# Where the attention matmuls stand among the feed-forward matmuls of the group before

## The chip, the cores and the metric

The kernel runs on one core of a Trainium2 chip. The core has five engines, each with its own in-order instruction queue: PE (TensorE, matrix multiply), DVE (VectorE), ACT (ScalarE), POOL (GpSimd) and SP (SyncE, which issues most of the DMAs). Time is device microseconds (us) of one execution, and lower is better. A scheduler writes the order of each engine's queue before the program runs. On the chip an engine takes its instructions in that order, and one that waits holds up everything queued behind it.

## The reference

A linear attention with a complex decay per channel is followed by a two-layer feed-forward block:

```python
for t in range(S):                       # S = 768, batch 4, heads 8, head_dim 48
    S_re, S_im = ar*S_re - ai*S_im + k[t] (x) v[t], ar*S_im + ai*S_re
    y[t] = q[t] @ S_re                   # a_re, a_im are first scaled to magnitude <= 0.999
x = y as (3072 tokens, 384 channels)
h = x @ w_in                             # 384 x 2048
out = max(0.01*h, h) @ w_out             # 2048 x 384
```

All data is float32, and the arrays w_in and w_out enter the kernel as float64 words.

## The kernel before, in words

The 768 positions are cut into 6 chunks of 128 tokens. One chunk of two batches is a *pass*, so there are 12 passes, numbered 0 to 11 (`SUBS`). For each pass the kernel does three things.

*Prep* (lines 438 to 611) is elementwise work on DVE and ACT: the magnitudes, the running products of the decay (lines 489 and 492, then 506 to 513), and their application to q and k. It writes `qkt`. Line 533 is the first write into the `qkt` of a pass and line 584, done twice, is the last. Ten DMAs (lines 600, 604 and 608) then carry `qkt` into `t96`, in a layout by head; the profile and its rows call this tile `t`. There is one `qkt` and one `t96` for all passes. So line 533 of the next prep has to wait until the DMAs have read `qkt`, and the DMAs of a pass have to wait until the attention of the pass before has finished with `t96`; its last reader there is the scaling of the state on ACT, line 729. In passes 0 and 1 five of the ten DMAs are issued by ACT, later all ten by SP.

*Attention* (`attend`, lines 632 to 733) has four pieces for a pass, scores and update for each of the two batches. A scores piece multiplies on PE from `t96` into PSUM; DVE then masks the result twice (line 670, tile `asb`). An update piece multiplies `asb` and the state into the attention's result, which ACT and DVE split into a high and a low part (`xh`, line 698, and `xl`, line 701), and updates the state (lines 722 and 729).

*Feed-forward* works on *groups* of 256 tokens, one for each pass. `first(g, s)`, for s from 0 to 7, is 18 matmuls into a PSUM tile `ph` (of which there are two), after which ACT, DVE, ACT and DVE make `tg`, `gh` and `gl` (lines 752 to 755). `second(g, s)` is 18 matmuls of `gh` and `gl` into `po`. Below, each such call of 18 matmuls is called a *step*, so a group has 16 steps. After the last, ACT copies `po` to `ot`, which SP stores (line 779).

While the feed-forward of group n-1 runs, the attention of pass n is put in between. The order on PE is fixed: every matmul is told to keep the order in which the program names it (`mm`, line 307). That order is made by this loop, in which `order` is the list of the steps of group n-1 and `pieces` the four attention pieces of pass n:

```python
805         if n > 0:
806             order = stream(n - 1)
807             for i, (what, g, s) in enumerate(order):
808                 what(g, s)
809                 left = len(order) - 1 - i
810                 while pieces and left <= GAP * len(pieces) + TAIL[min(n, len(TAIL) - 1)]:
811                     pieces.pop(0)()
812                     if left > 0:
813                         break
...
817         for p in pieces:
818             p()
```

`stream(g)` gives first 0, 1, 2, then second s-3 and first s alternating, then the last seconds. For groups 2 to 10 the last two seconds (6 and 7) are put behind first 0 of the next group. With `GAP` 2 the four pieces are issued two steps apart, and `TAIL[n]` says how many steps before the end of the group they begin. A value of -100 is never reached, so that the four pieces come after the last step of the group.

On the other engines the scheduler decides. It takes what is ready by its own simulation, attention before feed-forward before prep (`PRIO_ATT`, `PRIO_MOE`, `PRIO_PREP`), and fixes the order that comes out. In the first passes the weights are also converted, on DVE, ACT and POOL (`load_weights`, lines 406 to 434). In the last passes the weights are read once more and checked (`check_weights`, lines 392 to 404, tiles `wck`).

Of the kernel before, what the change touches and what calls it, by code (L numbers as in the profile page):

```python
# [42 lines left out]
OVERLAP = range(2, 11)  # L43

GAP = 2
TAIL = [0, -100, -100, 0, 2]
STAGES = [
    ("a", 3 * TI * 2 * C, 2), ("kn", H * 2 * D, 1), ("xh", TI * GT, 2), ("xl", TI * GT, 2), ("xh", TI * GT, 2),
    ("xl", TI * GT, 2), ("stg", 2 * DM, 1),
# [231 lines left out]
def body(ctx, tc, keep, a_in, qk_in, v_in, w_in, out):  # L281
# [512 lines left out]
    for n in range(nsub + 1):  # L794
# [10 lines left out]
        if n > 0:  # L805
            order = stream(n - 1)
            for i, (what, g, s) in enumerate(order):
                what(g, s)
                left = len(order) - 1 - i
                while pieces and left <= GAP * len(pieces) + TAIL[min(n, len(TAIL) - 1)]:  # L810
                    pieces.pop(0)()
# [86 lines left out]
```

## Time and profile before

| | us |
|---|---|
| median of 3 runs | 708.95 |
| lowest and highest | 705.37, 710.87 |
| the profiled execution | 711.76 |
| its span | 710.0 |
| PE busy | 563.7 (79%) |
| DVE busy | 550.4 (78%) |
| ACT busy | 366.2 (52%) |
| POOL busy | 79.2 (11%) |

The span is what the profiler saw between the first and the last instruction, and the profiled execution is 1.8 us longer than it. It lies 2.8 us above the median of the runs. A row of the timeline gives the start, the duration, the engine, the line, the operation and the count, and in brackets the idle time of that engine just before, with what ended it. A row of the waits gives who waited for whom, the sum, the number of times and the longest. A row of the windows gives the busy time of PE, of its weight load, of DVE, ACT and POOL in that stretch, the granted clock of PE as a share of full speed (PEclk), and the share of DMA time.

### The profile page before, as it was taken

The page shows a single profiled execution, that of the slowest core. Times are in us where ns is not written, and L with a number is a line of the kernel's source. Part 1 is how long each engine was busy: PE and PEld are TensorE (multiplying, and loading weights), DVE is VectorE, ACT ScalarE, POOL GpSimd, SP SyncE. Part 2 cuts the span into 40 slices and gives each one's busy share as a digit, 9 for nine tenths or more (in the row PEclk, how much of TensorE's full clock was granted, in tenths as well). Part 3 has the DMA queues.
Part 4 walks back from the last instruction along what each step waited for, and adds up shares of the span by engine and source line. Part 5 has one row for each costly group of instructions (what it writes and reads, how often), then busy time and mean ns, then how long its engine had stood idle before and what let it go on. Part 6 is the DMA issues. An engine that isn't in the chain of part 4 may idle for free.

```text
span 710.0 us, 17654 instructions
## 1 busy us (share of the span) xinstructions
PE 563.7 (79%) x7554; PEld 542.9 (76%) x7554; DVE 550.4 (78%) x917; ACT 366.2 (52%) x827; POOL 79.2 (11%) x75
## 2 busy tenths in 40 slices
PE   1000448966979889899899998998999979879996
PEld 0000338855978879889899998998999979879996
DVE  5999899999799599699896997969969767233331
ACT  6354276446453555464644755546456557554331
POOL 5645344630000000000000000000000000000000
PEclk9999956967989999999999999999999998989999
DMA  9222832720803503508025053160350674781000
GB/s 340 84 90 66 240 118 94 163 107 24 225 3 113 140 2 143 110 2 222 29 98 132 24 171 81 48 182 24 115 116 24 222 189 152 209 268 42 23 1 28
DMA packets 26247, 79.22 MB, mean 112 GB/s; under 512 B 3377, under 2 KB 9521, under 8 KB 26161
## 3 DMA queue, kind: packets, MB, share of 16 engines
q1 hardware_dynamic: 25552, 76.43, 36.3%
q10 hardware_dynamic: 608, 1.59, 1.0%
q8 instruction: 61, 1.00, 0.6%
q14 instruction: 26, 0.20, 0.1%
HBM read 54.26 MB, written 4.72 MB: 83 GB/s over the span
## 4 chain that ended last, share of the span: by engine, by line
DVE 41%; DMA 19%; PE 19%; ACT 7%; issue 7%; SPq 5%; POOL 1%; DVEq 0%; ACTq 0%
DMA t<-qkt 12%; PE po L308 8%; PE ph L308 6%; DMA wck<-in_w_dram 5%; PE att L308 4%; DVE tmp L489 3%; DVE gl L755 3%; DVE tg L753 3%; DVE asb L670 3%; DVE a L538 3%; ACT rst L729 2%; DVE a L492 2%; SPq L600 2%; DVE wcv L424 2%; SPq L604 2%
## 5 line engine op out<-in xcount | busy, mean ns | idle before, releaser
L308 PE MATMUL ph<-xh,win_hi 128*128 128x256 f32 x576 | 172.7, 300 | 26.8 <-DVE tg L753 20.0
L308 PE MATMUL ph<-xl,win_hi 128*128 128x256 f32 x576 | 167.7, 291 | 3.4 <-DVE xl L701 3.4
L308 PE MATMUL ph<-xh,win_lo 128*128 128x256 f32 x576 | 167.3, 290 | 2.0 <-POOL win_lo L434 2.0
L308 PE MATMUL po<-gh,wout_hi 128*128 128x256 f32 x576 | 144.0, 285 | 5.9 <-ACT ot L778 3.8
L308 PE MATMUL po<-gh,wout_lo 128*128 128x256 f32 x576 | 143.3, 284 | 0.0
L308 PEld LDWEIGHTS ph<-xh,win_hi 128*128 128x128 f32 x576 | 113.8, 198 | 31.9 <-DVE tg L753 22.0
L308 PEld LDWEIGHTS ph<-xl,win_hi 128*128 128x128 f32 x576 | 113.9, 198 | 4.2 <-DVE xl L701 4.2
L308 PEld LDWEIGHTS po<-gh,wout_hi 128*128 128x128 f32 x576 | 111.1, 193 | 6.5 <-ACT ot L778 4.0
L308 PEld LDWEIGHTS ph<-xh,win_lo 128*128 128x128 f32 x576 | 113.9, 198 | 2.5 <-POOL win_lo L434 2.5
L308 PEld LDWEIGHTS po<-gh,wout_lo 128*128 128x128 f32 x576 | 111.2, 193 | 0.0
L753 DVE TENSOR_TENSOR tg<-ph,tg 128x512 f32<-128x512 f32 x96 | 65.5, 684 | 48.8 <-ACT tg L752 46.2
L308 PE MATMUL att<-t 96*32 96x96 f32 (+3 forms) x1536 | 40.7, 261 | 76.3 <-DMA t<-qkt 73.4
L308 PEld LDWEIGHTS att<-t 96*32 96x32 f32 x1536 | 35.8, 146 | 80.6 <-DVE a L492 72.5
L754 ACT CAST gh<-tg 128x512 fp32r<-128x512 f32 x96 | 59.2, 617 | 53.8 <-DVE tg L753 50.9
L308 PE MATMUL po<-gl,wout_hi 128*128 128x256 f32 x576 | 84.5, 282 | 1.9 <-DVE gl L755 1.6
L755 DVE TENSOR_TENSOR gl<-tg,gh 128x512 fp32r<-128x512 f32 x96 | 68.2, 711 | 22.7 <-ACT gh L754 22.5
L752 ACT ACTIVATE tg<-ph 128x512 f32<-128x512 f32 x96 | 56.5, 589 | 43.2 <-PE ph L308 40.3
L308 PEld LDWEIGHTS po<-gl,wout_hi 128*128 128x128 f32 x576 | 75.5, 190 | 2.7 <-DVE gl L755 2.7
L533 DVE TENSOR_TENSOR qkt<-a 128x1536 f32<-128x1536 f32 x12 | 22.4, 1869 | 43.6 <-DMA t<-qkt 36.7
L489 DVE TENSOR_TENSOR tmp<-a 128x384 f32<-128x384 f32 x84 | 52.2, 622 | 1.3
L308 PE MATMUL att<-asb,v 128*32 128x128 f32 x768 | 43.3, 312 | 8.8 <-DVE asb L670 8.6
L729 ACT ACTIVATE rst<-rst,t 96x48 f32<-96x48 f32 x128 | 30.7, 323 | 20.2 <-DVE rst L722 20.1
(119 smaller groups left out, 898.9 us busy)
## 6 DMA issues: line engine op xcount, KB each, us to landing
t<-qkt SPq DMA_DIRECT2D x44, 290.2 KB, 6.0
wck<-in_w_dram SPq DMA_DIRECT2D x10, 1152.0 KB, 5.6
v<-in_v_dram SPq DMA_DIRECT2D x12, 832.0 KB, 4.7
a<-in_a_dram SPq DMA_DIRECT2D x12, 768.0 KB, 5.9
qk<-in_qk_dram SPq DMA_DIRECT2D x12, 768.0 KB, 4.4
out_dram<-ot SPq DMA_DIRECT2D x12, 384.0 KB, 2.6
stage_xh<-in_w_dram SPq DMA_DIRECT2D x10, 384.0 KB, 3.6
stage_xl<-in_w_dram SPq DMA_DIRECT2D x10, 384.0 KB, 3.0
```

Source lines behind the costliest of these rows:

```text
L308: tc.keep_in_program_order(nc.tensor.matmul(out, **kw))
L424: nc.vector.tensor_scalar(out=cv.bitcast(U32), in0=uwords[:, :, 1], scalar1=5, scalar2=2, op0=ALU.logical_shift_left, op1=ALU.logical_shif ...
L489: nc.vector.tensor_tensor(out=pr, in0=src.unsqueeze(2).to_broadcast([P, 2, 2, M]), in1=swap(ar, r), op=ALU.mult)
L492: nc.vector.tensor_tensor(out=zr[:, :, r], in0=pr[:, 0], in1=pr[:, 1], op=ALU.add)
L533: nc.vector.tensor_tensor(out=tb.rearrange("p l (r m) -> p l r m", r=R), in0=zl.rearrange("p l (r m) -> p l r m", r=R), in1=xt[:, 1].rearr ...
L538: nc.vector.tensor_tensor(out=zk, in0=zk, in1=over_r(0), op=ALU.mult)
L670: nc.vector.tensor_tensor(out=asb, in0=ps, in1=mask, op=ALU.mult)
L729: nc.scalar.activation(r[:, h // 2, h % 2], src[:, h // 2, h % 2], AF.Copy, scale=t96[:, s0 + x, bi, C : C + 1])
L752: nc.scalar.activation(tg, ph, AF.Copy, scale=0.01)
L753: nc.vector.tensor_tensor(out=tg, in0=ph, in1=tg, op=ALU.max)
L754: nc.scalar.copy(gh, tg)
L755: nc.vector.tensor_tensor(out=gl, in0=tg, in1=gh.bitcast(F32), op=ALU.subtract)
```

## The change

One line is changed, the table `TAIL`:

```diff
-TAIL = [0, -100, -100, 0, 2]
+TAIL = [1]
```

The table has one entry now, so every pass uses the value 1. This moves matmuls in all passes but pass 0:

- Passes 1 and 2: the four pieces stood behind all 16 steps of groups 0 and 1. They now stand after the steps with 9, 7, 5 and 3 steps left, which are first 4, 5, 6 and 7.
- Pass 3: they stood with 8, 6, 4 and 2 steps left, after second 1 to 4 of group 2, and now stand after first 3 to 6, one step earlier.
- Passes 4 to 11: they stood with 10, 8, 6 and 4 steps left, after second 0 to 3, and now stand after first 3 to 6, one step later.

No instruction's work changes. The order on the engines changes with the order on PE, since the scheduler works it out anew. Three places are shown, with a minus for a row of the kernel before, a plus for a row of the changed one.

The first is on DVE in the middle of group 0. The tile `a_2` belongs to the prep of pass 2, `wcv` to the weights, `tg_0_5` and `gl_0_5` to step first 5 of group 0, and `asb_1_0_0` is the first mask multiply of pass 1:

```order
 L755 TENSOR_TENSOR gl_0_4_928<-tg_0_4_926,gh_0_4_927 128x512
 L492 TENSOR_TENSOR a_2_756<-tmp_2_1318 128x2x96
-L753 TENSOR_TENSOR tg_0_5_970<-ph_0_5_951,tg_0_5_970 128x512
 L489 TENSOR_TENSOR tmp_2_1318<-a_2_756 128x384
 L492 TENSOR_TENSOR a_2_756<-tmp_2_1318 128x2x96
+L670 TENSOR_TENSOR asb_1_0_0_949<-att1_100,mask_78 128x512
 L489 TENSOR_TENSOR tmp_2_1318<-a_2_756 128x384
 L424 TENSOR_SCALAR wcv_30_457<-stage_stg_8_131 128x384
-L755 TENSOR_TENSOR gl_0_5_972<-tg_0_5_970,gh_0_5_971 128x512
 L492 TENSOR_TENSOR a_2_756<-tmp_2_1318 128x2x96
```

The mask multiply of pass 1 now stands where the feed-forward's step 5 stood, ahead of the last weights and of the rest of prep 2.

The second is on SP, the loads and stores around the `t96` of passes 2 and 3 (`ot` are the results of a group, `qk`, `a` and `v` the inputs of a pass):

```order
 L379 DMA a_3_1398<-in_a_dram 128x1536
-L779 DMA out_0_dram<-ot_0_1119 128x3x256
-L384 DMA qk_3_1399<-in_qk_dram 128x1536
-L379 DMA a_4_2074<-in_a_dram 128x1536
 L387 DMA v_2_758<-in_v_dram 128x1664
+L779 DMA out_0_dram<-ot_0_1313 128x3x256
 L600 DMA t96_2_1387<-qkt_2_1360 48x1548 x2
 L604 DMA t96_2_1387<-qkt_2_1360 32x2x516
```

The loads of `qk` and `a` that stood ahead of the DMAs into `t96` now stand behind them, and the store of group 0 stays ahead of those of pass 2. For pass 3 the store of group 1 now stands between the first two of the ten and the rest.

The third is on DVE around line 533 of prep 7, which runs beside group 5. Before:

```order
L512 TENSOR_TENSOR xs_7_4683<-tmp_7_4657 128x48
L513 TENSOR_TENSOR xs_7_4683<-tmp_7_4657 128x48
L533 TENSOR_TENSOR qkt_7_4699<-a_7_4061 128x2x768
L469 SCALAR_TENSOR_TENSOR tmp_8_5333<-tmp_8_5333 128x768
L753 TENSOR_TENSOR tg_5_0_4088<-ph_5_0_4069,tg_5_0_4088 128x512
L538 TENSOR_TENSOR a_7_4061<-a_7_4061 128x1536
L755 TENSOR_TENSOR gl_5_0_4090<-tg_5_0_4088,gh_5_0_4089 128x512
```

And now:

```order
L753 TENSOR_TENSOR tg_5_2_4181<-ph_5_2_4162,tg_5_2_4181 128x512
L506 TENSOR_TENSOR tmp_7_4657<-xs_7_4683 128x192
L512 TENSOR_TENSOR xs_7_4683<-tmp_7_4657 128x48
L513 TENSOR_TENSOR xs_7_4683<-tmp_7_4657 128x48
L755 TENSOR_TENSOR gl_5_2_4183<-tg_5_2_4181,gh_5_2_4182 128x512
L533 TENSOR_TENSOR qkt_7_4699<-a_7_4061 128x2x768
L469 SCALAR_TENSOR_TENSOR tmp_8_5333<-tmp_8_5333 128x768
L670 TENSOR_TENSOR asb_6_0_0_4251<-att1_100,mask_78 128x512
L538 TENSOR_TENSOR a_7_4061<-a_7_4061 128x1536
L753 TENSOR_TENSOR tg_5_3_4228<-ph_5_3_4209,tg_5_3_4228 128x512
```

The DVE work of firsts 0, 1 and 2 of group 5 (`tg` and `gl`), which was queued behind line 533, now stands ahead of it, and the mask multiplies of pass 6 (`asb_6`) stand two instructions behind it.

## The prediction

> **What bounds the kernel now.** The page comes first, then the windows by stage.
>
> ```profile
> PE 563.7 (79%) x7554; PEld 542.9 (76%) x7554; DVE 550.4 (78%) x917; ACT 366.2 (52%) x827; POOL 79.2 (11%) x75
> 100.00:180.00 80.00, 59.74 (x662) 55.98 (x655) 78.70 (x114) 45.02 (x106) 27.72 (x22) 0.74 0.33 98
> 372.00:560.00 188.00, 181.51 (x2637) 176.90 (x2636) 162.01 (x282) 103.30 (x246) 0.00 (x0) 0.99 0.35 99
> ```
>
> Over the whole span PE and DVE look alike, but the stages differ. From 100 to 180 us DVE is busy 78.7 of 80 us and PE 59.7: DVE bounds there, with the weights, prep 2 and the feed-forward of group 0. From 372 to 560 us PE is busy 181.5 of 188 us, 97%, and DVE 162.0, 86%: PE bounds there, with small gaps. The waits over the whole program tell what makes the gaps:
>
> ```profile
> DVE qkt L533 <- DMA t<-qkt: 36.7, 8, 5.7
> PE ph L308 <- DVE tg L753: 20.0, 10, 3.9
> ```
>
> Eight times DVE stands at line 533 until the DMAs into `t96` have read `qkt`. What is queued behind line 533 waits too, a `tg` among it, and PE then waits for that `tg` before it may refill a `ph`. The timeline of PE dates the stages. The rows are starts: scores of pass 1, group 1, scores of pass 2, group 2, scores of passes 3, 4, 8, 9 and 10.
>
> ```profile
> 160.74 0.50 PE L308 MATMUL att<-t 96*32 96x128 f32 x11
> 178.41 0.58 PE L308 MATMUL ph<-xh,win_hi 128*128 128x256 f32 x1
> 221.34 0.33 PE L308 MATMUL att<-t 96*32 96x128 f32 x4
> 235.26 0.38 PE L308 MATMUL ph<-xh,win_hi 128*128 128x256 f32 x1
> 250.73 0.33 PE L308 MATMUL att<-t 96*32 96x128 f32 x4
> 296.01 0.33 PE L308 MATMUL att<-t 96*32 96x128 f32 x4
> 489.35 0.33 PE L308 MATMUL att<-t 96*32 96x128 f32 x4
> 534.81 0.33 PE L308 MATMUL att<-t 96*32 96x128 f32 x4
> 581.76 0.35 PE L308 MATMUL att<-t 96*32 96x128 f32 x6
> ...
> 208.66 2.13 PE ph L308 x18
> 210.80 2.12 PE po L308 x18
> ```
>
> The last two rows are from the chain of waits: an undisturbed step is 2.13 us. From one pass's scores to the next (16 steps and an attention) the kernel takes 45.46 us at its best (489.35 to 534.81). From the start of group 1 to that of group 2, the same work, it takes 56.85 (178.41 to 235.26). From scores 4 to scores 10 it takes 285.75, which is 47.6 a pass. What the change can win lies in these two differences: 11.4 us early, 2.2 us a pass later.
>
> **The change, place by place.** I follow the new order with durations of the rows. The sum is made against the profiled execution, 711.8 us.
>
> *Scores of pass 1 inside group 0.* PE now comes to them after first 4, where it began second 2 before.
>
> ```profile
> 129.06 0.28 PE L308 MATMUL po<-gh,wout_hi 128*128 128x256 f32 x1
> 139.34 0.59 ACTq L608 DMA_DIRECT2D t<-qkt  x1
> t<-qkt ACTq DMA_DIRECT2D x4, 32.2 KB, 4.7
> 139.72 0.36 DVE L492 TENSOR_TENSOR a<-tmp 128x192 f32<-128x192 f32 x1
> 80.23 2.50 PE L308 MATMUL att<-t 96*32 96x64 f32 x56 [1.37 <-DMA t<-qkt]
> 176.27 1.82 DVE L584 TENSOR_TENSOR qkt<-qk,a 128x768 f32<-128x768 f32 x2
> L701 DVE SCALAR_TENSOR_TENSOR xl<-att,xh 128x384 fp32r<-128x384 f32 x24 | 13.2, 549 | 6.7 <-ACT xh L698 6.7
> ```
>
> PE is there at 129.1. The last DMA into this `t96` is issued at 139.3 and lands, by the median, 4.7 later, at 144.0. So PE stands for 14.9 us, with the rest of group 0 queued behind. DVE comes to the new mask multiply at 139.4 (the L492 row's end less the 0.68 of the `tg` that is no longer ahead) and finds it ready at 145.3 (half a cold scores piece, 2.50/2, after the landing). It stands for 5.9 us, and prep 2 and the last weights are queued behind. DVE has no slack here, so they end later by this. Up to line 584 of prep 2 both orders hold the same steps' `tg` and `gl` and four mask multiplies; the new one has one L701 more, 0.5. Line 584 ends at 178.0 before (the row holds most of both calls), and so at 184.4.
>
> The last `gl` of group 0 stands seven short DVE rows, some 4.4 us, ahead of that end. So second 7 ends and group 1 starts at about 180.7, 2.3 later than before, but with no attention left to do alone behind group 1.
>
> *Scores of pass 2 inside group 1.* After seven steps and 0.7 us of wait for a `tg`, PE is there at 196.3.
>
> ```profile
> 196.83 1.76 DVE L533 TENSOR_TENSOR qkt<-a 128x1536 f32<-128x1536 f32 x1 [5.65 <-DMA t<-qkt]
> 218.88 1.81 DVE L584 TENSOR_TENSOR qkt<-qk,a 128x768 f32<-128x768 f32 x2
> 222.34 0.69 DVE L670 TENSOR_TENSOR asb<-att,mask 128x512 f32<-128x512 f32 x1 [1.37 <-PE att L308]
> 238.60 2.56 SPq L600 DMA_DIRECT2D t<-qkt  x2
> 249.38 1.76 DVE L533 TENSOR_TENSOR qkt<-a 128x1536 f32<-128x1536 f32 x1 [3.43 <-DMA t<-qkt]
> L670 DVE TENSOR_TENSOR asb<-att,mask 128x512 f32<-128x512 f32 x48 | 31.7, 680 | 5.4 <-PE att L308 5.4
> L722 DVE TENSOR_TENSOR rst<-att,rst 96x384 f32<-96x384 f32 x16 | 8.7, 544 | 0.0
> ```
>
> From the first issue of the ten DMAs (238.60) to the end of the wait at line 533 (249.38) are 10.8 us. Issued at 184.4, those of pass 2 land at 195.2, just ahead of PE: no wait. Their place on SP helps, since two loads that stood ahead now stand behind; what could hold them is the store of group 0, which is ready by 181.5. Group 1 with attention 2 inside is then one undisturbed pass, 45.46 less the 1.0 of wait in it: 180.7 + 0.7 + 44.5 = 225.9 is the start of group 2, against 235.26.
>
> *Scores of pass 3.* Prep 3 is next to be late. Between the ends of line 584 of preps 2 and 3 lie 42.7 us before, with 5.65 of idle at line 533. The new order puts four L670, one more L701 and two L722 in, 4.4, and I add one wait for scores like that at 222.34, 1.4. The idle goes: 184.4 + 42.7 - 5.65 + 4.4 + 1.4 = 227.2. The store of group 1 between its DMAs costs 0.4; landing is at 238.4. PE is there five steps after 225.9, at 236.5, and waits 1.9. Before it was there at 250.73, with one step more behind it: 250.73 - 238.4 - 2.13 = **10.2 us gained**.
>
> *From scores 3 to scores 4.* 45.28 us before, for 14 steps and an attention; two steps less than the best pass would be 41.2. Of **4.1** I count all, since the waits of PE in it are for mask multiplies behind prep, which now stand ahead of it.
>
> *Scores 4 to scores 10.* These passes move by one step only.
>
> ```profile
> 416.50 0.30 PE L308 MATMUL att<-v,kn 128*32 128x48 f32 x9
> 433.12 1.76 DVE L533 TENSOR_TENSOR qkt<-a 128x1536 f32<-128x1536 f32 x1 [4.92 <-DMA t<-qkt]
> 436.40 0.39 PE L308 MATMUL ph<-xh,win_hi 128*128 128x256 f32 x1 [1.83 <-DVE tg L753]
> ```
>
> The attention ends on PE at 417.3, `t96` is free and filled 15.8 later, and PE has eight steps, 17.0, before the step that needs the `tg` behind line 533: it waits 1.83. In the new order `tg` and `gl` of firsts 0 to 2 stand ahead of line 533, and PE has ten steps, 21.3, before the next scores. So this wait should go. At the best row all six passes would win 285.75 - 6 x 45.46 = 13.0. Other waits will partly take its place on a DVE that is busy 86%. I take half, **6.5**. The other end: if the `tg` still waits, one step less covers it, and each pass loses 2.13, in all 12.8.
>
> *Clock.* New waits of PE cool it.
>
> ```profile
> 300.38 0.39 PE L308 MATMUL ph<-xh,win_hi 128*128 128x256 f32 x1 [2.35 <-DVE tg L753]
> 300.60 0.28 PE L308 MATMUL ph<-xl,win_hi 128*128 128x256 f32 x1
> ...
> 483.38 0.46 PE L308 MATMUL ph<-xh,win_hi 128*128 128x256 f32 x1 [2.13 <-DVE tg L753]
> 483.63 0.42 PE L308 MATMUL ph<-xl,win_hi 128*128 128x256 f32 x1
> 487.14 0.28 PE L308 MATMUL po<-gh,wout_hi 128*128 128x256 f32 x1
> ```
>
> After 2.35 us of wait matmuls ran at full speed, and after 2.13 another time at half (0.42 against 0.28), so that the step took 3.76 instead of 2.13. The wait of 1.9 at scores 3 can cost that difference, **1.6 lost**; the cold clock after scores 1 is hidden, since PE waits for DVE there anyway. The Trainium skill (TensorE: Matmul & The Clock Gate, Part 1) says that the clock falls to half only after an idle window of some 3.4 us, and speaks against any order with longer waits on PE. By it the wait at scores 3 would cost nothing and the sum would be 1.6 lower; the row after 2.13 us disagrees, and I go by the row.
>
> *The end.* The last passes share ACT with the weight check.
>
> ```profile
> PE po L308 <- ACT ot L778: 3.8, 1, 3.8
> ACT wck L403 <- DMA wck<-in_w_dram: 29.2, 9, 6.9
> ```
>
> On SP one `wck` load moves from ahead of the last `t96` to behind it, and its ACT row moves too. That may take away the 3.8 or add a wait as long as the longest, 6.9. I take 0.
>
> **Sum.** 10.2 + 4.1 + 6.5 - 1.6 = 19.2, so the profiled execution would take 692.5. It lay 2.8 above the median of the runs, so I forecast **690** (689.7). Best end: no wait at scores 3 (1.9 and 1.6 more), 13.0 instead of 6.5, 3.8 at the end, 33.0 in all: 676.
>
> **The rivals.** *No change.* The later passes lose what the early ones win. The `tg` of the step that PE needs is again stuck behind line 533, and the attention ends one step later than before, so that every pass loses 2.13. For it: the wait at line 533 comes eight times. Against it: the order shows three pairs of `tg` and `gl` moved ahead. 711.8 - 12.7 + 12.8 is 711.9, at the level of the median 709.
>
> *Slower: DVE becomes the bound at the mask multiply.* In the new order the L670 rows stand before the prep that the next pass needs. If the scores are not ready when DVE comes to one, DVE stands, prep is late, and `t96` is late for the next scores. Busy 86% of 47.6 us, DVE has 41.0 of work a pass. Two waits like the 5.9 at scores 1, one for each batch, make the pass 52.8, 5.2 more in each of seven passes: 711.8 - 12.7 + 36.4 = 735.5, at the level of the median 733. It cancels the gain from 4.2 us for each wait and is slower by 1% from 4.7. For it: my own working has that wait once. Against it: later `t96` is filled 15.8 us after the attention's end and PE comes 21.3 after it, so 5.5 are to spare.
>
> That the change does nothing is excluded by the order of the rows.
>
> **How the numbers follow.** Forecast 0.67, no change 0.15, slower 0.18. About 1%, 7 us, is what a measurement here tells from no change. The forecast's own range is 676 to 702 (without the 6.5 and with 6.9 lost at the end it is 703). The range is 676 to 715: it takes in the rival of no change and the smaller sizes of the slower one. Faster by over 1% 0.67, within 1% 0.15, slower 0.18.
>
> **What would show it.** Right: a wait of about 15 us of PE for `t` in front of the first scores of pass 1; one of about 6 us of DVE at L670 for PE; group 2 starting near 226; scores 4 near 285; the sum of L533 waits well below 36.7 and of `ph` waits for `tg` well below 20.0; passes of 45 to 47 us. Wrong: `ph` waits for `tg` once a pass, longer than 1.83 (no change); L670 waiting for PE in every pass, with passes over 49 us (slower); group 2 starting after 232, which would mean that DVE lost more than 5.9 in group 0.

## The result, and the profile after

The changed kernel takes 678.36 us in the median (678.07 to 679.77, four runs), beside 707.95 for the kernel before on the same chip (705.37 to 710.87, four runs). The ratio is 0.9585, with a 95% interval of 0.9543 to 0.9627. That is 29.6 us less; 19 were forecast. The profiled execution has a span of 678.0 us, 32.0 less than before.

First the page and the windows of the changed kernel, the same two stretches as before:

```profile
PE 544.5 (80%) x7554; PEld 526.7 (78%) x7554; DVE 548.2 (81%) x917; ACT 368.6 (54%) x827; POOL 83.3 (12%) x75
100.00:180.00 80.00, 56.30 (x690) 52.80 (x683) 76.12 (x110) 45.31 (x108) 27.49 (x22) 0.83 0.35 104
372.00:560.00 188.00, 179.51 (x2624) 175.39 (x2623) 165.11 (x285) 107.65 (x250) 0.00 (x0) 0.98 0.41 110
```

DVE does the same 548 us of work. PE is busy 19 us less with the same 7,554 matmuls; its mean granted clock is 0.964, where it was 0.939. From 372 to 560 us PE is not busier than before (179.5 against 181.5): one long wait lies in this stretch. The waits over the whole program:

```profile
PE ph L308 <- DVE tg L753: 13.1, 5, 6.5
DVE qkt L533 <- DMA out_dram<-ot: 9.3, 2, 6.3
DVE asb L670 <- PE att L308: 7.1, 3, 3.5
DVE qkt L533 <- DMA t<-qkt: 4.4, 2, 3.0
```

Two of the waits at line 533 are put down to a store (`out_dram<-ot`). The kernel before has one of them too:

```profile
DVE qkt L533 <- DMA out_dram<-ot: 6.5, 1, 6.5
```

Line 533 touches no `ot`, and these waits, too, end just behind the landing of the last DMA out of `qkt`: at 500.38 for a landing at 500.01, and in the kernel before at 295.43 for 295.11. So I count them with the waits for `t`. The 43.2 us in which DVE stood at line 533 for DMAs have become 13.7, and the 20.0 of `ph` for `tg` have become 13.1, of which 6.5 are a single wait. The timeline of PE dates the stages: scores of pass 1, group 1, scores 2, group 2, scores 3, then scores 4, 5, 8, 9 and 10, with the long wait ahead of scores 9:

```profile
140.09 0.64 PE L308 MATMUL att<-t 96*32 96x128 f32 x8 [10.55 <-DMA t<-qkt]
142.38 2.52 PE L308 MATMUL att<-t 96*32 96x64 f32 x56 [1.65 <-DMA stage_xh<-in_w_dram]
177.45 0.28 PE L308 MATMUL ph<-xh,win_hi 128*128 128x256 f32 x1
192.88 1.39 PE L308 MATMUL att<-t 96*32 96x128 f32 x55
221.84 0.28 PE L308 MATMUL ph<-xh,win_hi 128*128 128x256 f32 x1
232.59 0.44 PE L308 MATMUL att<-t 96*32 96x128 f32 x8
234.19 1.37 PE L308 MATMUL att<-t 96*32 96x64 f32 x56 [1.16 <-DMA t<-qkt]
278.16 1.53 PE L308 MATMUL att<-t 96*32 96x128 f32 x64
322.28 1.52 PE L308 MATMUL att<-t 96*32 96x128 f32 x64
455.31 1.53 PE L308 MATMUL att<-t 96*32 96x128 f32 x64
505.33 0.58 PE L308 MATMUL ph<-xh,win_hi 128*128 128x256 f32 x1 [6.54 <-DVE tg L753]
509.47 1.73 PE L308 MATMUL att<-t 96*32 96x128 f32 x62
554.49 1.53 PE L308 MATMUL att<-t 96*32 96x128 f32 x64
```

And the timeline of DVE: the mask multiply in group 0, the end of prep 2, and line 533 with the two `tg` behind it at the long wait:

```profile
143.63 0.69 DVE L670 TENSOR_TENSOR asb<-att,mask 128x512 f32<-128x512 f32 x1 [3.49 <-PE att L308]
179.12 1.81 DVE L584 TENSOR_TENSOR qkt<-qk,a 128x768 f32<-128x768 f32 x2
500.38 1.76 DVE L533 TENSOR_TENSOR qkt<-a 128x1536 f32<-128x1536 f32 x1 [6.33 <-DMA out_dram<-ot]
504.59 1.28 DVE L753 TENSOR_TENSOR tg<-ph,tg 128x512 f32<-128x512 f32 x2
```

Scores 4 to scores 5 take 44.12 us, and 278.16 to 455.31 is four such passes of 44.3 on average, 1.2 less than the best pass of the kernel before. The pass from scores 8 to scores 9 takes 54.2: DVE stands 6.33 us at line 533, the `tg` behind it comes at 504.59, and PE has waited 6.54 us for it at 505.33.

The 32.0 us come out by place like this. A step that is done earlier or later than before counts 2.13.

| place | working | measured | forecast |
|---|---|---|---|
| to scores 3 | 250.73 - 232.59 - 2.13 | 16.0 | 10.2, less 1.6 for the clock |
| scores 3 to 4 | 45.28 - (45.57 - 2 x 2.13) | 4.0 | 4.1 |
| scores 4 to 10 | 285.75 - 276.33 | 9.4 | 6.5 |
| scores 10 to the end | 128.24 - (123.51 + 2.13) | 2.6 | 0 |

### The profile page after: what moved, and what is told of

Read it like the earlier page. It is cut to its first block, busy times and chain, and to the rows that moved or that the text cites. A ratio compares the mean times of both kernels' runs of the same rounds, so it can differ in the third digit from the quotient of the medians.

```text
span 678.0 us, 17666 instructions
## 1 busy us (share of the span) xinstructions
PE 544.5 (80%) x7554; PEld 526.7 (78%) x7554; DVE 548.2 (81%) x917; ACT 368.6 (54%) x827; POOL 83.3 (12%) x75
## 4 chain that ended last, share of the span: by engine, by line
DVE 38%; PE 26%; DMA 18%; issue 6%; ACT 6%; POOL 2%; SPq 1%; ACTq 0%; DVEq 0%; POOLq 0%
PE ph L308 11%; PE po L308 11%; DMA t<-qkt 10%; DMA wck<-in_w_dram 5%; PE att L308 4%; DVE tg L753 3%; DVE gl L755 3%; DVE tmp L489 3%; DVE asb L670 2%; DVE qkt L584 2%; DVE wcv L424 2%; DVE a L483 2%; DVE a L538 2%; DVE qkt L572 2%; DVE a L492 2%
## 5 line engine op out<-in xcount | busy, mean ns | idle before, releaser
L308 PE MATMUL ph<-xh,win_hi 128*128 128x256 f32 x576 | 165.2, 287 | 13.5 <-DVE tg L753 13.1
L308 PE MATMUL ph<-xl,win_hi 128*128 128x256 f32 x576 | 164.5, 286 | 3.5 <-DVE xl L701 3.5
L308 PE MATMUL ph<-xh,win_lo 128*128 128x256 f32 x576 | 164.0, 285 | 0.0
L308 PE MATMUL po<-gh,wout_hi 128*128 128x256 f32 x576 | 146.2, 290 | 3.4 <-ACT gh L754 3.4
L308 PEld LDWEIGHTS ph<-xh,win_hi 128*128 128x128 f32 x576 | 110.7, 192 | 15.0 <-DVE tg L753 14.1
L308 PEld LDWEIGHTS ph<-xl,win_hi 128*128 128x128 f32 x576 | 110.8, 192 | 4.0 <-DVE xl L701 4.0
L308 PE MATMUL att<-t 96*32 96x64 f32 (+3 forms) x1536 | 41.4, 261 | 89.2 <-DMA t<-qkt 85.7
L308 PEld LDWEIGHTS ph<-xh,win_lo 128*128 128x128 f32 x576 | 110.8, 192 | 0.0
L754 ACT CAST gh<-tg 128x512 fp32r<-128x512 f32 x96 | 59.3, 619 | 51.4 <-DVE tg L753 50.4
L755 DVE TENSOR_TENSOR gl<-tg,gh 128x512 fp32r<-128x512 f32 x96 | 67.2, 700 | 12.1 <-ACT gh L754 11.9
L308 PE MATMUL att<-asb,v 128*32 128x128 f32 x768 | 39.4, 287 | 5.7 <-DVE asb L670 5.7
L670 DVE TENSOR_TENSOR asb<-att,mask 128x512 f32<-128x512 f32 x48 | 32.1, 679 | 7.1 <-PE att L308 7.1
L729 ACT ACTIVATE rst<-rst,t 96x48 f32<-96x48 f32 x128 | 30.7, 323 | 13.1 <-DVE rst L722 13.0
```

What stands on the lines that cost most here:

```text
L308: tc.keep_in_program_order(nc.tensor.matmul(out, **kw))
L670: nc.vector.tensor_tensor(out=asb, in0=ps, in1=mask, op=ALU.mult)
L729: nc.scalar.activation(r[:, h // 2, h % 2], src[:, h // 2, h % 2], AF.Copy, scale=t96[:, s0 + x, bi, C : C + 1])
L754: nc.scalar.copy(gh, tg)
L755: nc.vector.tensor_tensor(out=gl, in0=tg, in1=gh.bitcast(F32), op=ALU.subtract)
```

## The experiments

In all of them the start of each pass is read from PE's timeline. "Scores 4 to 10" is the time of six passes: 285.75 us in the kernel before, 276.33 in the changed one.

### One part of the table at a time

The early entries alone, and the late ones alone:

```diff
-TAIL = [0, -100, -100, 0, 2]
+TAIL = [0, 1, 1, 0, 2]
```

> Only passes 1 and 2 are spread; passes 3 to 11 stay where they were. Theory A (two separate gains, as the traces of before and after split them: 16.0 us until the scores of pass 3 and 4.0 to those of pass 4, then 9.4 and 2.6 from the later passes): some 20 us faster than before, 688; passes from scores 4 to scores 10 still near 47 us with waits of PE for tg behind line 533. Theory B (the later passes only follow from being ahead early; their shift by one step does nothing): about 30 us faster, 678, with later passes of 44 to 45 us.

```diff
-TAIL = [0, -100, -100, 0, 2]
+TAIL = [0, -100, -100, 1]
```

> Passes 1 and 2 stay behind their groups; passes 3 to 11 stand as in the changed kernel. Theory A: 10 to 14 us faster than before, 694 to 698, with group 2 starting near 235 as before, and passes of 44 to 45 us from scores 4 on. Theory B: no change, within 3 us of before.

The early entries alone took 673.2 us (ratio 0.9518, 0.9454 to 0.9581). That is somewhat less than the whole change, but the intervals overlap. The late entries alone took 717.13 (1.0121, 1.005 to 1.0193): slower. Theory A, two separate gains, falls. Theory B holds for the first kernel; for the second it expected no change, and the kernel lost 8 us. In the kernel with the early entries alone no pass from 3 on stands elsewhere among the steps than before, and still its passes are short. Its PE timeline, scores 4 and 6, and line 533 of two preps on DVE:

```profile
273.24 1.53 PE L308 MATMUL att<-t 96*32 96x128 f32 x64
361.68 1.53 PE L308 MATMUL att<-t 96*32 96x128 f32 x64
...
280.16 1.75 DVE L533 TENSOR_TENSOR qkt<-a 128x1536 f32<-128x1536 f32 x1
321.27 1.76 DVE L533 TENSOR_TENSOR qkt<-a 128x1536 f32<-128x1536 f32 x1 [0.54 <-ACT a L521]
```

361.68 - 273.24 are two passes of 44.2 us, with no wait for `t` at line 533. With the late entries alone, the PE timeline shows what the shift by one step does (two of five such waits, one a pass):

```profile
394.77 0.58 PE L308 MATMUL ph<-xh,win_hi 128*128 128x256 f32 x1 [3.16 <-DVE tg L753]
443.38 0.39 PE L308 MATMUL ph<-xh,win_hi 128*128 128x256 f32 x1 [2.89 <-DVE tg L753]
```

These are the waits of the kernel before, grown longer: the five behind line 533 of preps 7 to 11 take 17.9 us, and took 8.3 before (1.83 of it at 436.40). My account is that the attention ends a step later, `t96` is filled later, and the `tg` behind line 533 comes later.

### Each early pass by itself

```diff
-TAIL = [0, -100, -100, 0, 2]
+TAIL = [0, 1, -100, 0, 2]
```

> Only pass 1 is spread over group 0. Theory A1 (what wins early is that attention 2 no longer stands alone behind group 1, while pass 1 only exchanges one wait for another: group 1 started at 178.41 before and at 177.45 after): within 3 us of before. Rival A2 (the end of attention 1 releases the t96 of pass 2, so pass 1 carries the early gain): 10 us or more faster, with line 533 of prep 3 several us earlier than 196.83.

```diff
-TAIL = [0, -100, -100, 0, 2]
+TAIL = [0, -100, 1, 0, 2]
```

> Only pass 2 is spread over group 1. Theory A1: 13 to 18 us faster than before, group 2 starting near 226, with a wait of some 3 us at the scores of pass 2, since their t96 landed at 196.5 before. Rival A2: 5 us or less, since the t96 of pass 2 still waits for attention 1 behind group 0 and PE then stands for it inside group 1.

Pass 1 alone took 706.26 us (0.9975, 0.9939 to 1.001), pass 2 alone 702.39 (0.9923, 0.9887 to 0.9959). Both together had won 35.6. Theory A1 holds for the first of these kernels and fails for the second, where it expected 13 to 18 us; rival A2 fails for the first, and its 5 us or less come near the 6.4 of the second. So neither of the two passes owns the gain, and with either alone the later passes stay as slow as before (287.5 and 285.7 us from scores 4 to 10). The waits with pass 1 alone are those of the kernel before, a little fewer (6 for 8, and 9 for 10):

```profile
DVE qkt L533 <- DMA t<-qkt: 28.2, 6, 5.8
PE ph L308 <- DVE tg L753: 18.5, 9, 3.9
```

What tells these kernels apart is the order that the scheduler wrote for DVE. The table counts the `tg` multiplies and the mask multiplies that are queued ahead of line 533 of a prep:

| kernel | prep 4 | prep 5 | prep 6 | prep 8 | scores 4 to 10, us |
|---|---|---|---|---|---|
| before | 18, 12 | 25, 16 | 33, 20 | 48, 28 | 285.8 |
| late entries alone | 18, 12 | 25, 16 | 33, 20 | 49, 28 | 292.5 |
| pass 1 alone | 19, 12 | 25, 16 | 33, 20 | 48, 28 | 287.5 |
| pass 2 alone | 19, 12 | 26, 16 | 33, 20 | 48, 28 | 285.7 |
| both early passes | 20, 14 | 28, 18 | 35, 22 | 50, 28 | 272.5 |
| the change | 21, 14 | 28, 18 | 36, 22 | 50, 28 | 276.3 |

Where both early passes are spread, line 533 of preps 4 to 6 stands two or three `tg` later, behind half of the next attention's masks. This gave a new theory, C: the later passes are long where line 533 stands ahead of the `tg` that PE needs before its next scores, and waits there for `t96` to be filled. The next runs were meant to test both halves of it, the filling and the place.

### The filling: half of the DMAs issued by ACT

```diff
-            eng = nc.scalar if l == 1 and n < 2 else nc.sync
+            eng = nc.scalar if l == 1 else nc.sync
```

> The kernel before, but in every pass half of the DMAs into t96 (those of l = 1) are issued by ACT instead of SP. Theory C, the loop at line 533: in the kernel before the ten DMAs take SP some 10 us to issue (327.38 to 336.73 in its trace), line 533 stands until they have landed, and the tg that PE needs stands behind it. With two queues the landing comes 3 to 5 us earlier, so the 36.7 us of waits at line 533 for t fall below 15, the 20.0 us of ph waiting for tg fall below 10, and the six passes from scores 4 to scores 10 go from 47.6 to 45 to 46 us: 692 to 698 us. Theory D, the landing is only a symptom and the later passes are long because their attention has too many waits of its own: within 4 us of the kernel before, the ph waits for tg stay, and the five issues on ACT (3 to 6 us a pass) may make it a little slower.

It took 693.22 us (0.9767, 0.9738 to 0.9796), the time that theory C gave, with 276.9 from scores 4 to 10. Its waits:

```profile
PE ph L308 <- DVE tg L753: 5.4, 4, 2.6
DVE qkt L533 <- DMA t<-qkt: 1.2, 1, 1.2
```

Both waits are nearly gone, and 16 us with them. The passes are still 46.2 on average, and PE now waits 11.0 us in all for `gh` of ACT, where it waited 2.0. But the filling did not become shorter, as theory C had it. From the first issue of the ten DMAs of a pass to the landing of the last it took 12.1 us, in the mean of passes 3 to 10, where the kernel before took 11.6. What the edit did change is the order of DVE: line 533 of preps 4, 5, 6 and 8 now has 19, 27, 35 and 49 `tg` ahead of it, where it had 18, 25, 33 and 48. From prep 5 on it comes up 1.7 to 4.3 us after the landing. So this run does not test the filling apart from the place; it is one more kernel in which line 533 stands later and its wait is gone. The same edit on the kernel with both early passes spread:

> TAIL = [0, 1, 1, 0, 2] (attention of passes 1 and 2 spread, all else as before) with half of the DMAs into t96 issued by ACT. Theory C: the passes of 44.2 us up to scores 8 are PE's own floor and stay; what is left are the waits at line 533 of preps 8 to 10 (8.6 and 3.1 us) and passes of 47.0, 48.6 and 50.3 us, of which 3 to 6 us go: 667 to 670. Theory D: no gain, 672 to 676.

It took 678.01 us (0.9553, 0.9529 to 0.9577), not 667 to 670, and not the 672 to 676 of theory D either. The interval overlaps that of the kernel without the edit (0.9454 to 0.9581): there is no gain, and a loss is not shown. The filling takes 12.6 us with the edit and without it. Line 533 no longer waits for a DMA there. But now ACT is late. Rows of ACT (its own issues are ACTq) and of PE in the same few us:

```profile
532.26 1.69 ACTq L604 DMA_DIRECT2D t<-qkt  x1
539.89 3.39 ACTq L608 DMA_DIRECT2D t<-qkt  x2
543.32 0.62 ACT L754 CAST gh<-tg 128x512 fp32r<-128x512 f32 x1 [8.73 <-DMA t<-qkt]
...
543.99 0.39 PE L308 MATMUL po<-gh,wout_hi 128*128 128x256 f32 x1 [4.33 <-ACT gh L754]
```

The last two of ACT's five issues come 5.9 us behind the third and take 3.39, and `gh`, queued behind them, starts 8.73 us after the instruction ahead of it on ACT. PE waits 4.33 us for it. The trace shows what the two issues came behind. The one at 539.89 begins 0.02 us after the landing of a load, that of `v`, which SP had issued at 526.92; the other, at 542.69, begins 0.02 us after the landing of a DMA into `t96` that SP had issued at 530.71. So here an issue on ACT stood until a DMA issued by SP had landed, and ACT's own work stood behind it. What a shorter filling would be worth neither run shows, since in neither did it become shorter.

### The place of line 533

Here `TAIL` stays as in the kernel before, but line 533 of prep m is tied to the second mask multiply of pass m - 1, by a copy of one column of its result into the scratch that line 533 overwrites:

```diff
+    tok = keep.tile([P, nsub], F32, tag="tok", name="tok")
...
+        if n > 2:
+            nc.vector.tensor_copy(out=tb[:, 0, 0:1], in_=tok[:, n - 1 : n])
...
                 am.append(asb)
+                if bi == 0 and hh == 1:
+                    nc.vector.tensor_copy(out=tok[:, n : n + 1], in_=asb[:, 0, 0:1])
```

> The kernel before with nothing of its TAIL changed, but from prep 3 on line 533 of prep m is made to come behind the second mask multiply of pass m - 1 (a one-column copy of that result into the scratch that line 533 overwrites). In the order of DVE line 533 of preps 4, 5 and 6 then has 20, 27 and 35 tg and 14, 18 and 22 mask multiplies ahead of it, as in the kernel with passes 1 and 2 spread (20, 28, 35 and 14, 18, 22), where the kernel before has 18, 25, 33 and 12, 16, 20. Theory C, the place of line 533 decides the later passes: the waits at line 533 for t go, the ph waits for tg go, passes from scores 4 to scores 10 fall from 47.6 to 44.2 to 45.5 us (13 to 20 us less): 689 to 696 us. Theory F, its place only follows from PE being further ahead: a prep that starts later ends later, t96 lands later, the scores wait for t instead, and the time is within 5 us of the kernel before or above it.

It took 689.87 us (0.9739, 0.9693 to 0.9786), with 272.1 us from scores 4 to 10, as in the kernel with both early passes spread (272.5). Here line 533 is number 536, line 670 is 673 and line 753 is 758. Its waits at this line and of `ph` for `tg`, then line 533 of one prep with the masks ahead of it, and scores 4 and 10:

```profile
PE ph L308 <- DVE tg L758: 6.6, 3, 3.0
DVE qkt L536 <- ACT a L524: 1.2, 2, 0.9
...
337.02 1.35 DVE L673 TENSOR_TENSOR asb<-att,mask 128x512 f32<-128x512 f32 x2
339.52 1.76 DVE L536 TENSOR_TENSOR qkt<-a 128x1536 f32<-128x1536 f32 x1
...
291.82 1.53 PE L308 MATMUL att<-t 96*32 96x128 f32 x64
563.95 1.53 PE L308 MATMUL att<-t 96*32 96x128 f32 x64
```

No wait for `t` is left at this line: from prep 4 on it comes up 5.1 to 10.4 us after the landing. The filling itself takes longer than before, 13.1 us in the mean of passes 3 to 10 (11.6), so it is the place and not the filling that ended the wait. The masks ahead of it need the scores, the scores need `t96`, and the DMAs that fill `t96` are the ones that line 533 waits for: when it comes up they are done. Theory F, that the place only follows, falls: behind pass 0 the scores wait for `t` at most 2.8 us in all. With no matmul moved on PE the later passes have the length that the early entries gave them.

The same tie on the two faster kernels, where line 533 had gone back to its old place from prep 7 or 8 on:

> TAIL = [0, 1, 1, 0, 2] with the same tie of line 533 to the mask multiplies of the pass ahead. It changes the order for preps 7 to 11 alone, where line 533 again stood ahead of them (43, 50, 57 tg and 25, 28, 32 masks for preps 7 to 9; now 43, 51, 59 and 26, 30, 34). Theory C: the passes of 47.0, 48.6 and 50.3 us from scores 8 on shorten to 44.2 to 46, 8.6 and 3.1 us of wait at line 533 go: 664 to 670. Theory F: 672 to 680.

> The changed kernel with the same tie. Theory C: the pass of 54.2 us from scores 8 to scores 9, with its wait of 6.54 us for the tg behind line 533, becomes one of 44 to 46, and the time 666 to 672. Theory F: 676 to 684, with PE waiting for t in front of the scores of passes 8 to 10.

With the early entries alone it took 670.64 us (0.9475, 0.9437 to 0.9513), at the edge between the two theories. Two of the three passes from scores 8 on became shorter there (45.8 and 46.1 us, for 47.0 and 48.6), the third did not (50.4 for 50.3). With the whole change it took 668.18 (0.9449, 0.941 to 0.9487), as theory C gave. The latter has the lowest median here, and its interval lies below that of the change. Scores 8, 9 and 10 on its PE timeline:

```profile
453.10 1.53 PE L308 MATMUL att<-t 96*32 96x128 f32 x64
497.99 1.53 PE L308 MATMUL att<-t 96*32 96x128 f32 x64
543.92 1.53 PE L308 MATMUL att<-t 96*32 96x128 f32 x64
```

The pass of 54.2 us, with its wait of 6.54, is one of 44.9 now.

### Which half of the step shift costs

```diff
-TAIL = [0, 1, 1, 0, 2]
+TAIL = [0, 1, 1, 1, 2]
```

> TAIL = [0, 1, 1, 1, 2]: passes 1 and 2 spread, and pass 3 one step earlier as in the changed kernel, passes from 4 on where they were before. It tells which half of the step shift makes the changed kernel some 5 us slower than the one with passes 1 and 2 alone (673.2). If the shift of pass 3 costs (its trace has 2.8 us more than two steps account for between scores 3 and 4), 675 to 677; if only the later passes do, 672 to 674.

```diff
-TAIL = [0, 1, 1, 0, 2]
+TAIL = [0, 1, 1, 0, 1]
```

> TAIL = [0, 1, 1, 0, 1]: passes 1 and 2 spread, pass 3 where it was before, passes from 4 on one step later as in the changed kernel. If a pass that begins one step later has one step less of cover at the next line 533, the later passes cost what they cost with the early passes left alone or a part of it, among it a wait of 5 us or more for tg near scores 9: 676 to 680. If the shift of pass 3 is what costs: 672 to 674.

677.02 us (0.9555, 0.9531 to 0.958) and 677.83 (0.9555, 0.9519 to 0.9592). By the medians each half costs about 4 us, but they don't add up: the whole change took 678.36. The intervals overlap that of the early entries alone (0.9454 to 0.9581), so I leave this undecided. The trace is clear on one thing: the long wait at scores 9 belongs to the shift of the later passes. It is there in the second kernel and not in the first:

```profile
502.90 0.58 PE L308 MATMUL ph<-xh,win_hi 128*128 128x256 f32 x1 [5.89 <-DVE tg L753]
```

With the tie no cost of the shift is seen (668.2 with it, 670.6 without).

### Pass 1 alone, with the tie

> TAIL = [0, 1, -100, 0, 2] (pass 1 alone spread) with the tie of line 533, beside 689.9 for the kernel before with the tie and 706.3 for pass 1 alone without it. Pass 1 alone brought scores 2 from 221.34 to 211.73, 9.6 us, of which 1.3 were left at scores 3. Theory G, it was lost at line 533 of prep 3, which fell back to its old place: with the tie most of the 9.6 reach the end, 679 to 685 us. Theory H, it was lost since attention 2 still stands alone behind group 1, where PE waits for DVE anyway: 686 to 691 us, and only both passes together give the early gain.

684.6 us (0.9626, 0.9571 to 0.9682), just inside what theory G gave. At scores 3 it is 5.7 us ahead of the tied kernel before (242.13 against 247.78), and 4.9 in the span (683.1 against 688.0). So part of what pass 1 wins had been lost at line 533. But with both early passes and the tie the span is 669.2, 18.8 less than 688.0. Pass 2 thus brings another 13.9 by the spans once pass 1 is spread. The runs are from two chips; by the ratios, each beside the kernel before on its own chip, pass 1 brings some 8 us and pass 2 some 11. Without the tie pass 2 alone won 6.4. No run has pass 2 alone with the tie, so whether the two still help each other there is not shown.

## Why the prediction was right, and where it was not

The time lay in the range, some 12 us below the forecast. By the steps:

*What bounds the kernel.* Right, and the runs show it twice: without the waits at line 533 (half of the DMAs on ACT, or the tie) the unchanged order of matmuls becomes 16 to 17 us faster.

*Scores 1.* PE was forecast to stand for 14.9 us until 144.0 and stood 10.55 until 140.09 and then 1.65 more. The last DMA into this `t96` was issued at 140.06 (forecast 139.3) and landed 4.2 us later, at 144.21, near the 144.0 of the forecast. The step that was wrong is that the scores wait for it. They began at 140.09, when a first part had landed (140.04), ran on at 142.38, and only the last of them stood until the last landing:

```profile
144.26 0.23 PEld L308 LDWEIGHTS att<-t 96*32 96x32 f32 x8 [0.29 <-DMA t<-qkt]
```

So DVE stood 3.49 at line 670 and not 5.9, line 584 of prep 2 ended at 180.9 and not 184.4, and group 1 started at 177.45, where 180.7 was forecast: earlier than before and not later.

*Scores 2 and 3.* No wait at scores 2, as forecast, at 192.88. Group 2 at 221.84 (forecast 225.9), scores 3 at 232.59 with a wait of 1.16 in it (forecast 238.4 with 1.9). The gain of 10.2 was mis-sized: it was 16.0. Of the 5.8 us, 2.1 are the same wrong step again, since scores 3 began 2.1 ahead of the last landing into their `t96` (234.70). The other 3.7 are that this landing came earlier than forecast, behind a prep 2 that had ended 3.5 earlier.

*Clock.* The term of 1.6 did not come: behind the wait of 1.16 the scores ran at full speed (1.37 for 56, against 2.50 in the cold row at 80.23). By the rule of the Trainium skill that was weighed there (TensorE: Matmul & The Clock Gate, Part 1) nothing was to be lost, and so it came. (By it the gains would have summed to 20.8; it is the time that would have been 1.6 lower, not the sum.) The wait, though, was shorter than forecast, so this place doesn't decide between rule and row; the last section has rows that do.

*Scores 3 to 4.* 4.0 for 4.1.

*Scores 4 to 10.* The size was near (9.4 for 6.5), and the mechanism half right. That the `tg` moves ahead of line 533 and ends the wait is what the tie shows. But I put this down to the shift by one step of the later passes, and it is the early passes that make the scheduler write it. The shift alone does what my rival of no change says, and costs 8 us. With the early entries alone these six passes win 13.3, of which 3.8 are missing in the change, so that 9.4 came near my 6.5 is luck. The step that failed is that I took early and late entries as separate terms of a sum: pass 1 (-2.5 us), pass 2 (-6.4) and the late entries (+8) by themselves don't add up to the -29.6 of all together. The best end was also too careful: a pass can take 44.1 us, not 45.46, since even the best pass before held a wait.

*The end.* 2.6 for 0, within its ends. The slower rival did not come: line 670 waited for PE three times in all, 7.1 us.

Open is by which of its rules the scheduler puts line 533 later when both early passes are spread. The runs show that its place decides, not why it was chosen.

## What to carry to other kernels

Where a scheduler writes the queues, an edit in the first stages may change the order of all later ones, so read the order around the wait that ends last in each stage, not only around the edit. In an in-order queue the place of an instruction that waits for a DMA can matter more than how long the DMA takes: put it behind the work that another engine needs next. Where every edit makes the scheduler write a new order, look whether a test changed only what it was meant to change: the split of the DMAs moved line 533 as well. Before adding up the gains of two parts of a change, ask whether one of them decides where the other one's wait stands.

## What the hardware showed that was not expected

The clock after a wait of PE does not go by the length of the wait alone. The PE timeline of the kernel with the late entries alone, with the first matmul behind two waits and the one after it:

```profile
443.38 0.39 PE L308 MATMUL ph<-xh,win_hi 128*128 128x256 f32 x1 [2.89 <-DVE tg L753]
443.60 0.28 PE L308 MATMUL ph<-xl,win_hi 128*128 128x256 f32 x1
...
490.46 0.58 PE L308 MATMUL ph<-xh,win_hi 128*128 128x256 f32 x1 [2.77 <-DVE tg L753]
490.84 0.41 PE L308 MATMUL ph<-xl,win_hi 128*128 128x256 f32 x1
```

The longer wait was followed by full speed (granted clock 1.00 from 443.38 to 446.00), the shorter one by matmuls of 0.41 us (0.50 from 490.46 to 493.00). In the changed kernel the clock fell only after PE had been back at work for 1.1 us:

```profile
590.94 0.38 PE L308 MATMUL po<-gh,wout_hi 128*128 128x256 f32 x1 [2.20 <-ACT gh L754]
591.16 0.28 PE L308 MATMUL po<-gh,wout_lo 128*128 128x256 f32 x1
...
591.95 0.28 PE L308 MATMUL po<-gh,wout_hi 128*128 128x256 f32 x1
592.07 0.38 PE L308 MATMUL po<-gh,wout_lo 128*128 128x256 f32 x1
592.24 0.42 PE L308 MATMUL po<-gh,wout_hi 128*128 128x256 f32 x1
```

The granted clock is 1.00 from 590.94 to 592.00 and 0.50 from 593.00 to 595.00. So the clock is not decided at the wait itself. The page of the Trainium skill named above says in the same part that activity is judged in windows of some 3.4 us that run freely, and the late fall agrees with that. Its other statement, that a whole idle window must pass before the clock falls, does not hold here: 2.77 us of wait were enough at 490.46. How much idle time in a window it takes was not measured.
